# Transposing three token tiles by DMA instead of by matmul, with one mixer tile and two statistics moved, in an attention and mixer kernel

## The chip, the cores and the metric

The kernel runs on one core of one Trainium2 chip. The metric is the device time of one execution in microseconds; the median of three runs is given, and one more execution was taken by the hardware profiler. The engines are called PE (TensorE, matmuls), PEld (its weight loads), DVE (VectorE), ACT (ScalarE), POOL (GpSimd) and SP (SyncE, which here only issues DMAs; SPq is its queue).

## The reference

The input x has 2048 tokens of 512 channels. It is normalised, and the normalised tokens go two ways: through attention over cached keys and values, and through a mixer with an MLP, whose result gates the attention's.

```python
def _A_ref(x, k_cache, v_cache, wq, wo):           # 32 heads of 128, 2048 keys
    q = (x @ wq).reshape(B, Sq, H, Dh)              # then heads first
    p = _softmax(einsum("bhqd,bhkd->bhqk", q, k_cache) * Dh ** -0.5)
    return einsum("bhqk,bhkd->bhqd", p, v_cache) ... @ wo

def _B_ref(x, w1, w2, w3, w4):
    h = _gelu(_layernorm(x) @ w1)
    # four groups of 128 channels, shifted by +1, -1, +2 and -2 tokens
    x1 = x + concatenate([g0, g1, g2, g3]) @ w2
    return x1 + _gelu(_layernorm(x1) @ w3) @ w4     # 512 -> 1792 -> 512

xn = _layernorm(x)
out = x + _A_ref(xn, ...) * _silu(_B_ref(xn, ...))
```

All arrays are bf16.

## The kernel before

Tokens are cut into 16 tiles of 128 (index t). The kernel has a prologue of about 130 us, which computes the whole mixer with the MLP apart from held-back pieces, and then the attention: 128 units (a head with 512 queries each) of eight slots, each slot a pair of score matmuls, an exponential on ACT, and the value matmuls of an earlier slot. The diff touches only the first 50 us of the prologue.

Every engine executes its own instructions in the order in which the program issues them (`pin` keeps it). DMAs of SP are issued in order too; each also waits until the DMA eight places before it has landed, since eight completion semaphores are used in turn. So the order of work is the order of the Python lines, per engine.

The prologue's steps, by their functions:

- `load_x(t)` (L163) loads a token tile into a buffer of the tag "ta", of which there are ten. Tiles 0 to 7 are loaded first, then the query weights of four heads, then w2, then tiles 8 to 15.
- `ln1(t, tr)` issues on DVE the statistics of tile t + 1 (L182, L183, with two small POOL operations, L177 and L178, for the inverse root) and the normalisation of tile t into `xall` (L187), and then calls `tr(t)`, which puts the tile's transpose into `xnT`.
- `tr_pe(t)` does that with four 128-column matmuls against an identity matrix into a PSUM buffer "ps_o", and a copy by ACT (L201). `tr_dma(t)` does it with one DMA transpose from `xall` to `xnT`, issued by SP (L204).
- `m1(c0, 512)` is the mixer's first matmul for four tiles at once: two PSUM buffers of 1024 columns, eight matmuls each, and a gelu on ACT into `hT` (L215). It reads the four tiles' columns of `xnT`. For tiles 0 to 3 `m1_tile` does the same tile by tile.
- `m2(t)` is the second matmul of a tile: four matmuls from `hT`, shifted by up to two tokens, into a "ps_o" buffer, of which there are two (pool psO). `x1(t, ps)` adds it to `xall` on DVE (L227), and frees the buffer.
- `q_ahead(u)` computes the queries of a unit ahead of the attention: four matmuls (`q_mm`) into a buffer of pool psX, "xa" or "xm" in turn by the length of the list `made`, and a copy by ACT (`q_copy`, L279). The units of the last heads use weights `wq_e`, which SP loads (L594) after the DMA transposes of tiles 8 to 15; the weights w3 follow (L596).
- `stats(xall, mv2, rs2, t)` are the second statistics, of the mixer's result, and `ln2(t)` normalises with them and issues a DMA transpose into `xn2T` (L235) for the MLP's first matmul `m3` (L244).

Before the change, tiles 0 to 7 are transposed by `tr_pe` and 8 to 15 by `tr_dma`; `tr_q` puts one query unit of the first four ahead of each of the transposes of tiles 4 to 7. All loads of tiles 8 to 15 are issued before that. On PE the order from there on is: m2 of tiles 0 and 1, m1(512), units 4 to 7, m2 of tiles 2 and 3, m1(1024), four units with `wq_e`, m2 of tiles 4 to 7, m1(1536), m2 of tiles 8 to 10, three units, m2 of tiles 11 to 15, and then m3. On DVE the second statistics of tiles 4 to 7 stand between the residual adds of tiles 10 and 11.

Of the kernel before, what the change touches and what calls it, by code (L numbers as in the profile page):

```python
# [10 lines left out]
FP32 = mybir.dt.float32  # L11
# [6 lines left out]
def kernel(  # L18
# [15 lines left out]
    nc = tc.nc  # L34
    P = nc.NUM_PARTITIONS
# [3 lines left out]
    Sq, D = x2d.shape  # L39
# [6 lines left out]
    DC = D // P  # L46
# [17 lines left out]
    def pool(name, bufs=1, space=None, **kw):  # L64
        if space is not None:
            kw["space"] = space
        return tc.tile_pool(name=name, bufs=bufs, **kw)
# [4 lines left out]
    xall = const.tile([P, NT, D], BF16, name="xall")  # L72
# [5 lines left out]
    mv2 = const.tile([P, NT, nc.vector.BN_AGGR_DIM], FP32, name="mv2")  # L78
    rs1 = const.tile([P, NT], FP32, name="rs1")
    rs2 = const.tile([P, NT], FP32, name="rs2")  # L80
# [12 lines left out]
    psO = ent(pool("psO", 2, PSUM))  # L93
    psX = ent(pool("psX", 1, PSUM))
# [14 lines left out]
    def mm(out, lhsT, rhs, start, stop):  # L109
        pin(nc.tensor.matmul(out=out, lhsT=lhsT, rhs=rhs, start=start, stop=stop))  # L110
# [50 lines left out]
    def load_x(t, eng):  # L161
        xin[t] = tokp.tile([P, D], BF16, tag="ta", bufs=10, name="xin")
        pin(eng.dma_start(out=xin[t][:], in_=xsrc[t]))  # L163
# [11 lines left out]
    def rsqrt(out, var):  # L175
        ve = smp.tile([P, 1], FP32, name="ve")
        pin(nc.gpsimd.tensor_scalar(out=ve[:], in0=var, scalar1=EPS, scalar2=None, op0=ALU.add))  # L177
        pin(nc.gpsimd.tensor_tensor(out=out, in0=ve[:], in1=nhalf[:], op=ALU.pow))  # L178

    def stats(src, mv, rs, t):  # L180
        bn = smp.tile([P, nc.vector.BN_STATS_DIM], FP32, name="bn")
        pin(nc.vector.bn_stats(out=bn[:], in_=src))  # L182
        pin(nc.vector.bn_aggr(out=mv[:, t, :], in_=bn[:]))  # L183
        rsqrt(rs[:, t:t + 1], mv[:, t, 1:2])

    def norm_to(out, src, mv, rs, t):
        pin(nc.vector.tensor_scalar(  # L187
            out=out, in0=src, scalar1=mv[:, t, 0:1], scalar2=rs[:, t:t + 1],
            op0=ALU.subtract, op1=ALU.mult))
# [7 lines left out]
    def tr_pe(t):  # L197
        tp = psO.tile([P, DC, P], FP32, tag="ps_o", name="ps_o")
        for dc in range(DC):
            mm(tp[:, dc, :], xall[:, t, dc * P:(dc + 1) * P], ident[:], True, True)  # L200
        pin(nc.scalar.activation(out=xnT[:, :, t * P:(t + 1) * P], in_=tp[:], func=ACT.Identity))  # L201
# [4 lines left out]
    def m1(c0, w):  # L206
        for jp in range(DC // 2):
            b = BASE_J[2 * jp]
            ps = psS.tile([P, 2, 512], FP32, name="ps_s")
            for j in range(2):  # L210
                jc = 2 * jp + j
                for dc in range(DC):
                    mm(ps[:, j, 0:w], w1_sb[:, dc, jc * P:(jc + 1) * P],
                       xnT[:, dc, c0:c0 + w], dc == 0, dc == DC - 1)
            pin(nc.scalar.activation(  # L215
                out=hT[:, 2 * jp:2 * jp + 2, b + c0:b + c0 + w], in_=ps[:, :, 0:w],
                func=ACT.Gelu_apprx_tanh))

    def m2(t):
        ps = psO.tile([P, D], FP32, tag="ps_o", name="ps_o")  # L220
        for jc in range(DC):
            c0 = BASE_J[jc] + t * P - SHIFT[jc]
            mm(ps[:], hT[:, jc, c0:c0 + P], w2_sb[:, jc, :], jc == 0, jc == DC - 1)
        return ps
# [4 lines left out]
    def ln2(t):  # L229
        c, ts = divmod(t, 4)  # L230
        if ts == 0:
            xn2T[c] = pL.tile([P, DC, 512], BF16, tag="xn2T", bufs=2, name="xn2T")
        y = tokp.tile([P, D], BF16, tag="ta", bufs=10, name="xn2")
        norm_to(y[:], xall[:, t, :], mv2, rs2, t)
        pin(nc.sync.dma_start_transpose(out=xn2T[c][:, :, ts * P:(ts + 1) * P], in_=y[:]))  # L235
# [30 lines left out]
    def q_mm(u, dcs, tag="xa"):  # L266
        g, qt, hh = units[u]
        if dcs[0] == 0:
            st[u] = dict(psq=psX.tile([P, 512], FP32, tag=tag, name="ps_q"))
        for dc in dcs:  # L270
            mm(st[u]["psq"][:], wqs[g * HG + hh][:, dc, :],
               xnT[:, dc, qt * 512:(qt + 1) * 512], dc == 0, dc == DC - 1)

    def q_copy(u, eng=None):
        qT = qtp.tile([P, 512], BF16, name="qT")
        if eng is None:
            pin(nc.vector.tensor_copy(out=qT[:], in_=st[u].pop("psq")[:]))  # L277
        else:
            pin(nc.scalar.activation(out=qT[:], in_=st[u].pop("psq")[:], func=ACT.Identity))  # L279
        st[u]["qT"] = qT  # L280
# [251 lines left out]
    def ln1(t, tr):  # L532
        if t + 1 < NT:
            ln1_stats(t + 1)
        ln1_norm(t)
        tr(t)
# [28 lines left out]

    made = []

    def q_ahead(u):
        q_mm(u, range(DC), ("xa", "xm")[len(made) % 2])
        q_copy(u, nc.scalar)  # L570
        made.append(u)

    def tr_q(t):
        q_ahead(t - 4)
        tr_pe(t)

    for t in range(8, 16):
        load_x(t, nc.sync)
    for t in range(4, 8):
        ln1(t, tr_q)  # L580
    pend = [(t, m2(t)) for t in range(2)]
    for t in range(8, 12):
        ln1(t, tr_dma)
    m1(512, 512)
    for t, ps in pend:
        x1(t, ps)
    for u in range(HG, 2 * HG):
        q_ahead(u)
    pend = [(t, m2(t)) for t in range(2, 4)]
    for t in range(12, 16):  # L590
        ln1(t, tr_dma)
    for h in range((NG - 1) * HG, NG * HG):
# [9 lines left out]
    for u in range(NU - 2 * HG, NU - HG):  # L602
        q_ahead(u)
    for t in range(4, 8):
        x1(t, m2(t))
    for t in range(4):
        ln2(t)
    m1(1536, 512)
    for t in range(8, 11):
        x1(t, m2(t))  # L610
    for u in (2 * HG, NU - 1, NU - HG):
        q_ahead(u)
    for t in range(4, 8):
        stats(xall[:, t, :], mv2, rs2, t)
    for t in range(11, 16):
        x1(t, m2(t))
# [109 lines left out]
    for v in range(1, NU):  # L726
        if v not in made:
            for dc in range(DC):
                k = dc - 1 if v - 2 >= TURN.start else dc // 2
                q_plan[(v - 1) * SPU + k].append((v, (dc,)))  # L730

    for n in range(UB * SPU):
        u, p = divmod(n, SPU)
# [81 lines left out]
    def bank(pl, tag, **kw):  # L815
        return pl.tile([P, D], FP32, tag=tag, name="ps_w", **kw)[:]
# [4 lines left out]
    ps = {ts: bank(psW, "w") for ts in (0, 1)}  # L821
# [83 lines left out]
```

## Time and profile before

| what | value |
|---|---|
| median of three runs | 1252.07 us (1251.08 to 1252.3) |
| profiled execution, its own time | 1249.84 us |
| span of the profiled execution | 1248.0 us |
| mean granted PE clock | 0.999 |
| busy PE, ACT, DVE, POOL | 1241.3, 1111.2, 1007.5, 35.4 us |
| DMA, mean | 85 GB/s |
| m1(512), m1(1024), m1(1536) start on PE | 17.57, 26.23, 36.71 us |
| m3 of the first 512 tokens starts on PE | 50.23 us |
| first DMA transpose of `xnT` issued by SP | 15.09 us |
| first `wq_e` load issued by SP | 26.11 us |

Times inside the profile count from the start of the span. A row of a timeline gives start, length, engine, line and operation; PE's matmuls are pipelined, so rows of PE overlap by some tenths of a microsecond, and the pace is read from start to start. The chain that ended last is followed back from the end through what released each step.

### The profile page before, as it was taken

The page shows a single profiled execution, that of the slowest core. Times are in us where ns is not written, and L with a number is a line of the kernel's source. Part 1 is how long each engine was busy: PE and PEld are TensorE (multiplying, and loading weights), DVE is VectorE, ACT ScalarE, POOL GpSimd, SP SyncE. Part 2 cuts the span into 40 slices and gives each one's busy share as a digit, 9 for nine tenths or more (in the row PEclk, how much of TensorE's full clock was granted, in tenths as well). Part 3 has the DMA queues.
Part 4 walks back from the last instruction along what each step waited for, and adds up shares of the span by engine and source line. Part 5 has one row for each costly group of instructions (what it writes and reads, how often), then busy time and mean ns, then how long its engine had stood idle before and what let it go on. Part 6 is the DMA issues. An engine that isn't in the chain of part 4 may idle for free.

```text
span 1248.0 us, 16327 instructions
## 1 busy us (share of the span) xinstructions
PE 1241.3 (99%) x5884; PEld 606.2 (49%) x5884; DVE 1007.5 (81%) x1452; ACT 1111.2 (89%) x1117; POOL 35.4 (3%) x91
## 2 busy tenths in 40 slices
PE   9999999999999999999999999999999999999998
PEld 5444444444444444444444444444444444444444
DVE  7621678888888888888888888888888989899887
ACT  5344989999999999999999999999999999999997
POOL 5310000000000000000000000000000000000000
PEclk9999999999999999999999999999999999999999
DMA  6582023454244523553235524363245523462222
GB/s 179 116 149 64 18 43 72 89 111 85 49 96 89 116 52 65 97 120 68 68 86 105 102 40 93 81 119 68 60 98 103 103 67 82 102 117 60 60 65 60
DMA packets 235825, 106.48 MB, mean 85 GB/s; under 512 B 187808, under 2 KB 219040, under 8 KB 235744
## 3 DMA queue, kind: packets, MB, share of 16 engines
q1 hardware_dynamic: 234224, 102.82, 40.0%
q0 software_dynamic: 672, 1.84, 0.8%
q8 instruction: 46, 0.75, 0.3%
q10 hardware_dynamic: 848, 0.79, 0.2%
q14 instruction: 35, 0.29, 0.1%
HBM read 67.90 MB, written 2.36 MB: 56 GB/s over the span
## 4 chain that ended last, share of the span: by engine, by line
PE 99%; DVE 1%; ACT 1%; issue 0%; ACTq 0%
PE ps_s L110 40%; PE ps_o L110 38%; PE ps_wo L110 9%; PE ps_q L110 8%; PE ps_m L110 2%; PE ps_warm L110 0%; PE ps_oh L110 0%; ACT qT L279 0%; DVE bn L182 0%; ACT tb L501 0%; ACT xnT L201 0%; PE ps_w L110 0%; PE ps_sum L110 0%; DVE y L404 0%; DVE xall L227 0%
## 5 line engine op out<-in xcount | busy, mean ns | idle before, releaser
L293 ACT ACTIVATE pT<-ps_s 128x1024 bf16<-128x1024 f32 x1016 | 1037.4, 1025 | 61.8 <-PE ps_s L110 11.5
L110 PE MATMUL ps_s<-qT,kT 128*128 128x512 bf16 (+1 forms) x2064 | 609.1, 377 | 0.0
L110 PE MATMUL ps_o<-pT,vb 128*128 128x512 bf16 x2032 | 603.5, 379 | 0.0
L304 DVE TENSOR_TENSOR acc<-acc,pT 128x2048 bf16<-128x2048 bf16 x254 | 307.7, 1211 | 97.3 <-ACT pT L293 96.2
L110 PEld LDWEIGHTS <-kT 128*128 128x128 bf16 x2064 | 232.9, 113 | 218.0
L110 PEld LDWEIGHTS <-vb 128*128 128x128 bf16 x2064 | 201.8, 98 | 224.0 <-issue 0.5
L110 PE MATMUL ps_wo<-wo_h,oT 128*128 128x512 bf16 x496 | 186.7, 379 | 0.0
L299 DVE TENSOR_TENSOR acc<-pT 128x2048 bf16<-128x2048 bf16 x127 | 155.3, 1223 | 36.0 <-ACT pT L293 35.6
L110 PE MATMUL ps_q<-xnT,wq_h 128*128 128x512 bf16 x488 | 180.1, 379 | 0.0
L365 DVE TENSOR_TENSOR oT<-ps_o,rb 128x512 bf16<-128x512 f32 x127 | 86.7, 682 | 10.1 <-DMA rb<-dr 10.0
L308 DVE TENSOR_TENSOR acc<-acc 128x1024 bf16<-128x1024 bf16 x127 | 87.9, 692 | 4.3
L110 PEld LDWEIGHTS <-oT 128*128 128x128 bf16 x508 | 56.7, 112 | 58.6 <-issue 0.2
L345 DVE TENSOR_REDUCE sm<-tT 128x4 f32<-128x512 bf16 x116 | 78.6, 678 | 1.2 <-DMA tT<-acc 0.9
L277 DVE CAST qT<-ps_q 128x512 bf16<-128x512 f32 x113 | 77.2, 683 | 0.0
L110 PEld LDWEIGHTS <-wq_h 128*128 128x128 bf16 x488 | 47.6, 98 | 56.7 <-issue 0.2
L423 DVE TENSOR_TENSOR sacc<-ps_wo,sacc 128x512 f32<-128x512 f32 x96 | 65.6, 684 | 4.5 <-PE ps_wo L110 4.4
L314 DVE TENSOR_TENSOR acc<-acc 128x512 bf16<-128x512 bf16 x126 | 53.6, 425 | 4.3
L244 ACT ACTIVATE h2T<-ps_s 128x1024 bf16<-128x1024 f32 x28 | 28.7, 1025 | 24.3 <-PE ps_s L110 24.3
L110 PE MATMUL ps_s<-xn2T,w_sb 128*128 128x512 bf16 x224 | 48.8, 379 | 0.0
L110 PEld LDWEIGHTS <-w_sb 128*128 128x128 bf16 x336 | 30.4, 98 | 32.1
L110 PEld LDWEIGHTS <-h2T 128*128 128x128 bf16 x224 | 21.9, 98 | 26.3
L110 PE MATMUL ps_m<-w_sb,h2T 128*128 128x512 bf16 x112 | 33.3, 379 | 0.0
(74 smaller groups left out, 337.7 us busy)
## 6 DMA issues: line engine op xcount, KB each, us to landing
rb<-dr SPq DMA_DIRECT2D x127, 256.0 KB, 3.9
vb<-in_A_v_cache_dram SPq DMA_DIRECT2D x64, 256.0 KB, 3.0
wq_h<-in_A_wq_dram SPq DMA_DIRECT2D x32, 128.0 KB, 3.1
wo_h<-in_A_wo_dram SPq DMA_DIRECT2D x32, 128.0 KB, 2.8
w_sb<-in_B_w_dram SPq DMA_DIRECT2D x8, 256.0 KB, 5.1
kT<-in_A_k_cache_dram SPq DMA_TRANSPOSE x128, 3.0
xl<-in_A_x_dram SPq DMA_DIRECT2D x16, 128.0 KB, 3.5
dr<-rc SPq DMA_DIRECT2D x127, 2.0 KB, 1.4
```

Of the source, the lines that this page charges most:

```text
L110: pin(nc.tensor.matmul(out=out, lhsT=lhsT, rhs=rhs, start=start, stop=stop))
L244: pin(nc.scalar.activation(out=h2[c, f][:], in_=ps[:], func=ACT.Gelu_apprx_tanh))
L277: pin(nc.vector.tensor_copy(out=qT[:], in_=st[u].pop("psq")[:]))
L293: pin(nc.scalar.activation(out=s["pT"][-1][:, jj:jj + 2, :], in_=sps[:], func=ACT.Exp, scale=SCALE))
L299: pin(nc.vector.tensor_tensor(out=s["acc"][:], in0=s["pT"][0][:], in1=s["pT"][1][:], op=ALU.add))
L304: pin(nc.vector.tensor_tensor(out=a[:], in0=a[:], in1=st[u]["pT"][i][:], op=ALU.add))
L308: pin(nc.vector.tensor_tensor(out=a[:, 0:2, :], in0=a[:, 0:2, :], in1=a[:, 2:4, :], op=ALU.add))
L314: pin(nc.vector.tensor_tensor(out=a[:, 0, :], in0=a[:, 0, :], in1=a[:, 1, :], op=ALU.add))
L345: pin(nc.vector.tensor_reduce(out=sm[:], in_=s["tT"][:], axis=mybir.AxisListType.X, op=ALU.add))
L365: pin(nc.vector.tensor_tensor(out=to, in0=o, in1=rb, op=ALU.mult))
L423: pin(nc.vector.tensor_tensor(out=sa, in0=ps[:], in1=sa, op=ALU.add))
```

## The change

Tiles 4, 5 and 6 are transposed by `tr_dma` in place of `tr_pe`; tile 7 stays with PE. Of the loads of tiles 8 to 15, which SP issued all together, tiles 8 to 11 are still issued at once, 12 and 13 behind the DMA transpose of tile 4, and 14 and 15 behind that of tile 5; the transpose of tile 6 follows, and then those of tiles 8 to 15. So SP issues three more DMAs, and PE runs units 0 to 3 back to back.

m2 of tile 2 moves ahead of m1(512), into the psX buffer "xa"; its residual add moves along. Units 4 to 7 take "xm" and "xa" in the other order (the argument k). The second statistics of tiles 4 and 5 move ahead of m1(1536) and of the residual adds of tiles 8 to 10; those of 6 and 7 stay where they were.

```diff
-    def m2(t):
-        ps = psO.tile([P, D], FP32, tag="ps_o", name="ps_o")
+    def m2(t, pl=psO, tag="ps_o"):
+        ps = pl.tile([P, D], FP32, tag=tag, name="ps_o")
...
-    def q_ahead(u):
-        q_mm(u, range(DC), ("xa", "xm")[len(made) % 2])
+    def q_ahead(u, k=0):
+        q_mm(u, range(DC), ("xa", "xm")[(len(made) + k) % 2])
         q_copy(u, nc.scalar)
         made.append(u)
 
+    more_x = {3: range(8, 12), 4: range(12, 14), 5: range(14, 16)}
+
     def tr_q(t):
         q_ahead(t - 4)
-        tr_pe(t)
-
-    for t in range(8, 16):
-        load_x(t, nc.sync)
+        (tr_dma if t < 7 else tr_pe)(t)
+        for k in more_x.get(t, ()):
+            load_x(k, nc.sync)
+
+    for k in more_x[3]:
+        load_x(k, nc.sync)
     for t in range(4, 8):
         ln1(t, tr_q)
     pend = [(t, m2(t)) for t in range(2)]
+    pend.append((2, m2(2, psX, "xa")))
...
     for u in range(HG, 2 * HG):
-        q_ahead(u)
-    pend = [(t, m2(t)) for t in range(2, 4)]
+        q_ahead(u, 1)
+    pend = [(3, m2(3))]
...
     for t in range(4):
         ln2(t)
+    for t in (4, 5):
+        stats(xall[:, t, :], mv2, rs2, t)
     m1(1536, 512)
...
-    for t in range(4, 8):
+    for t in (6, 7):
         stats(xall[:, t, :], mv2, rs2, t)
```

## The prediction, on record before the change was run

> **What bounds the kernel now.** I read the page first, then the chain of waits for the first 52 us (the diff touches nothing later), the timelines of TensorE (PE) and of SyncE's queue (SPq) there, and the DMA landings.
>
> ```profile
> PE 1241.3 (99%) x5884; PEld 606.2 (49%) x5884; DVE 1007.5 (81%) x1452; ACT 1111.2 (89%) x1117; POOL 35.4 (3%) x91
> PE 99%; DVE 1%; ACT 1%; issue 0%; ACTq 0%
> ```
>
> PE is the bound: 99% busy, 99% of the chain. So a microsecond of PE work or PE idling taken away in the prologue moves all that follows, and whatever ends later than PE wants it costs the same. PE's timeline (start, length; a row's length overlaps the next, so I count from start to start):
>
> ```profile
> 11.24 1.03 PE L110 MATMUL ps_q<-xnT,wq_h 128*128 128x512 bf16 x4
> 12.11 0.39 PE L110 MATMUL ps_o<-ident,xall 128*128 128x128 bf16 x4
> 12.33 1.03 PE L110 MATMUL ps_q<-xnT,wq_h 128*128 128x512 bf16 x4
> ...
> 15.62 2.11 PE L110 MATMUL ps_o<-w_sb,hT 128*128 128x512 bf16 x8
> 17.57 3.62 PE L110 MATMUL ps_s<-xnT,w_sb 128*128 128x512 bf16 x16
> ...
> 45.42 1.89 PE L110 MATMUL ps_o<-w_sb,hT 128*128 128x512 bf16 x8
> 47.56 2.83 PE L110 MATMUL ps_o<-w_sb,hT 128*128 128x512 bf16 x12 [0.25 <-DVE xall L227]
> ```
>
> Four transposing matmuls of one tile take 0.22 us of PE (12.11 to 12.33), a query unit 0.87 (11.24 to 12.11), and one tile of the second mixer matmul, m2, also 0.87 (four 512-column matmuls). The last row shows PE idle for 0.25 us for VectorE's (DVE's) residual add. The chain there shows why: four second statistics stand ahead of that add.
>
> ```profile
> 46.13 0.59 DVE bn L182
> ...
> 46.84 0.68 DVE xall L227
> ```
>
> SP's queue, and where a DMA transpose is priced (least/median/most ns of issue, then us from issue to landing):
>
> ```profile
> 8.47 3.99 SPq L163 DMA_DIRECT2D xin<-in_A_x_dram  x8
> 15.09 10.97 SPq L204 DMA_TRANSPOSE xnT<-xall  x8
> 26.11 2.22 SPq L594 DMA_DIRECT2D wq_e<-in_A_wq_dram  x4
> ...
> L204 SPq DMA_TRANSPOSE xnT<-xall x8: 1196/1216/1300, 15.1 to 24.8; - x8
> DMA to landing us min/median/max: 2.4/2.5/2.7
> ```
>
> SP issues in order: a transposed tile holds it 1.2 to 1.3 us, a plain load about 0.5 (eight in 3.99), and the four extra query weights wq_e stand behind all transposes.
>
> **Part one: tiles 4 to 6 leave PE.** Removed: 12 matmuls and three ACT copies. On PE that is 3 x 0.22 = 0.66 us. Bounds: nothing, if PE had waited there for ACT anyway; 3 x 0.39 = 1.17 by the rows' lengths. ACT does run without a pause there (0.60 and 0.49 us alternating, 1.09 a pair, equal to PE's pitch), but each query copy begins 0.03 us after its matmuls end, so PE leads: 0.66. The short wait of m2(1) for tile 7's ACT copy stays, since q(3), tile 7 and m2(0) follow each other as before.
>
> *When the three tiles arrive.* m1(512) reads tiles 4 to 7 at once, so the last, tile 6, is what counts. PE gets there at 17.57 + 0.87 (the m2 tile now ahead of it) - 0.66 = 17.78. SP: load 11 is issued at 10.03 in 0.38; tile 4 (normalised by 10.34) at 10.45 to 11.75; loads 12 and 13 to 12.75; tile 5 at 12.8 to 14.05; loads 14 and 15 to 15.0; tile 6 at 15.05, landing 2.5 later at 17.55. The margin is 0.2 us. The wait for the eighth DMA back doesn't bind: tile 5 waits for w2, landed at 12.1. Behind PE's wait for tile 6 everything on PE is queued.
>
> *DMA engines.* Three tiles issued at 15.09, 16.49 and 17.78 make a share of 0.49 in 16 to 20 us: 4 x 0.49 / 3 = 0.65 us of all engines each.
>
> ```profile
> 8.00:12.00 4.00, 4.00 (x64) 3.58 (x62) 3.90 (x10) 3.42 (x10) 3.13 (x8) 1.00 0.98 271
> 12.00:16.00 4.00, 4.00 (x32) 2.29 (x30) 3.86 (x12) 3.80 (x8) 3.04 (x8) 1.00 0.63 196
> ```
>
> The share (before the GB/s) leaves 0.08 + 1.48 = 1.56 us free by 16 us: room for tiles 4 and 5, with tile 6 after. But they queue behind w2 and the loads, in engines that are full until 12, so I call d what tile 6 is late beyond 15.05 + 2.5. Bounds for d: 0, and 4.6 from the slowest rows of any transpose in backlog:
>
> ```profile
> 64.80 3.54 SPq L235 DMA_TRANSPOSE xn2T<-xn  x1
> 79.76 1.76 SPq L235 DMA_TRANSPOSE xn2T<-xn  x1
> ```
>
> There the issue took 3.54 and 1.76 us instead of 1.22, that is 2.3 or 0.55 more, for each of two tiles ahead of tile 6. At 79.76 two plain loads of 256 KB stood ahead on the same queue, as w2 and x loads do here, and it landed 3.6 after its issue; at 64.80 fourteen loads from GpSimd's queue shared the engines, which none does here. I take d = 0.1, since SP issues loads every 0.5 us from 8.5 to 11.8 although the engines are full.
>
> *SP's queue behind it.* Loads 12 to 15 come up to 2.4 us later; DVE wants load 12 at 17.34 and has it by 16. Tiles 8 to 11 go out at 16.35 to 20.25, wanted at 25.6: covered. Tile 12 then waits for its DVE normalisation (20.91, and 0.62 later for a third residual add ahead of it: 21.5); tiles 12 to 15 at 21.55 to 25.45, the first wq_e at 26.7 instead of 26.11. It landed in 2.4: 29.1. PE's weight load wanted it at 29.47, and now at 28.81. So 0.3 us is paid there, and d moves it one for one; the next three have 0.1 to 0.6 of slack.
>
> **Part two: m2(2) ahead of m1(512), in psX.** The same four matmuls, moved; m2(3) alone stays behind. Its columns end in tile 3, whose gelu is done at 12.1. It holds the psX buffer "xa" until DVE's third add (about 20.4); the swapped parity gives the next query unit "xm", and "xa" is wanted at 22.1. Cost nothing; if that add were late, PE would pay the lateness.
>
> **Part three: statistics of tiles 4 and 5 ahead of m1(1536).** Two pairs of 0.8 us move to DVE's idle stretch before the add of tile 8 (2.33 us of idle at 41.23). Then the add of tile 11 follows its matmuls, and of the 0.25 us idle about 0.05 stays: -0.20. GpSimd's two small operations per tile move along, idle there from 31 to 44 us.
>
> **Sum.** -0.66 - 0.20 + 0.30 + 0.10 = -0.46 us. On the profiled execution (span 1248.0, own time 1249.84) that gives 1249.4; the median of the runs shown is 2.23 higher, 1252.07, so 1251.6. It is 0.04%; about 0.2%, 2.5 us, is what a measurement of this kernel can tell from no change.
>
> **Rivals.**
>
> *Late tiles, a small loss or no gain (0.20).* The price of 79.76 for tile 4 alone gives d = 0.55 and a sum of 0.0; for tiles 4 and 5 with a landing of 3.6, d = 2.2 and +1.6: 1252.1 to 1253.7. For it: the full engines. Against: 2.4 to 2.7 in all eight rows of L204. The Trainium skill (VectorE: DVE Perf Modes, The three transpose paths and Rules for kernel authors) speaks against this change: TensorE where PSUM will do, at 390 ns a block, and the DMA crossbar at 1309 ns only otherwise. By its figure a tile of four blocks would be an estimated 5.2 us, tile 6 would land at 20.3, and the time would be 1254.2; the trace has 2.5 us for a tile.
>
> *SP blocks, slower (0.09).* If the engines' backlog holds the issue of tiles 4 and 5 as at 64.80, d is 4.6: PE waits 4.4 us for m1(512) and 0.5 for wq_e, +4.0, 1256.1. It counts as slower from d = 3.1, tile 6 landing after 20.6. For it: three of the four issues of L235 from 63 to 73 us took long (3.54, 1.82, 2.90). Against: only with GpSimd's loads in the air.
>
> *All cover holds, more gain (0.12).* wq_e lands in time too, or the matmuls cost their rows' lengths: -0.86 to -1.4, so 1250.7 to 1251.2.
>
> *A transpose is dearer on PE than it looks (0.04).* Tile 0's four, the first, have a row of 0.63 us: three tiles then take 1.9, the sum is -1.7, 1250.4. The Trainium skill (TensorE: Matmul & The Clock Gate, Part 4: PE-mode transpose) gives about 275 ns for each block in a kernel; 12 of them, 3.3 us by estimate, make the sum -3.1 and the time 1249.0, faster by 0.25%. The trace's 0.055 each (0.22 for four) is against it.
>
> **How the numbers follow.** Forecast 0.55; with the late tiles and the held cover 0.87 within 0.2%. Slower 0.09 is the blocked SP. Faster 0.04 is the dear transposes, counted in full though their row stays under the bound. The range takes -1.4 and +1.6 and 0.6 for the scatter of the runs (1251.08 to 1252.3), cut at the thin upper end: 1250.0 to 1253.7.
>
> **What would show it.** Right: PE starts m1(512) near 17.8 to 17.9 and the first wq_e matmul near 29.3 (29.69 before), no idle of 0.25 before m2's last tiles, and the last gated tiles about 0.5 us earlier. Wrong: an L204 issue over 1.5 us or a landing over 3 among the first three, a PE wait for DMA of a microsecond at 18 us or 29 us, PE idle on "xa", or any new wait of PE after 52 us.

## The result, and the profile after

The changed kernel takes 1253.89 us (median of 21 runs, 1252.77 to 1255.65); the kernel before, run beside it, 1251.35 (21 runs, 1250.44 to 1252.82). The ratio is 1.0019 (95% interval 1.0013 to 1.0025, given in brackets from here on): slower by 2.5 us, at the edge of the 0.2% that the prediction called measurable, outside its range and with the other sign. The profiled execution has a span of 1250.8 us (before 1248.0) and an own time of 1252.77; its mean granted clock is 0.999. The profiled execution of the kernel before (1249.84) was faster than every one of these 21 runs of it, so what its profile doesn't show can still cost the median run something.

The page's busy times and the shares of the chain that ended last:

```profile
PE 1234.7 (99%) x5757; PEld 606.0 (48%) x5872; DVE 1006.3 (80%) x1452; ACT 1108.9 (89%) x1114; POOL 35.5 (3%) x91
...
PE 93%; DVE 3%; DMA 3%; issue 1%; ACT 1%; POOL 0%; SPq 0%; ACTq 0%
```

PE has 99% of the chain in the kernel before and 93% here: the chain now runs through DVE and DMAs. The list of PE's waits has two lines that the kernel before doesn't have and that matter here (columns: us in total, times, longest):

```profile
PE ps_o L110 <- DVE oT L365: 1.7, 3, 0.7
...
PE ps_s L110 <- DMA xnT<-xall: 0.9, 1, 0.9
```

The second is the wait for tile 6. The first, three waits, lies in the attention, 200 us and more behind everything that the diff touches; no such line is in the profile of before. The 2.8 us between the two spans divide so: 0.56 by the start of the gated MLP matmuls (m3, 50.79 against 50.23), 1.65 in the three waits of the first line, 0.3 spread over the rest of the attention, and 0.3 behind PE's last matmul.

**The prologue.** PE's timeline:

```profile
15.07 3.00 PE L110 MATMUL ps_o<-w_sb,hT 128*128 128x512 bf16 x12
18.99 3.61 PE L110 MATMUL ps_s<-xnT,w_sb 128*128 128x512 bf16 x16 [0.92 <-DMA xnT<-xall]
...
30.50 3.75 PE L110 MATMUL ps_q<-xnT,wq_e 128*128 128x512 bf16 x16
...
46.32 4.64 PE L110 MATMUL ps_o<-w_sb,hT 128*128 128x512 bf16 x20
50.79 1.46 PE L110 MATMUL ps_s<-xn2T,w_sb 128*128 128x512 bf16 x6
```

m2(0) starts at 15.07 against 15.62, although tile 0 was 0.15 late in this execution, so the removed transposes gave 0.70. Twelve m2 matmuls later m1(512) finds tile 6 missing, and starts at 18.99. Three m2 tiles at the pace of the kernel before take 2.82 (1.95 for two there, 0.87 for the third) and would end at 17.89, so the loss is 1.10. The row of m2's last tiles has no idle inside it any more. SP's queue shows why tile 6 was late:

```profile
10.53 1.29 SPq L204 DMA_TRANSPOSE xnT<-xall  x1
11.87 1.89 SPq L163 DMA_DIRECT2D xin<-in_A_x_dram  x2
13.86 1.20 SPq L204 DMA_TRANSPOSE xnT<-xall  x1
15.11 1.05 SPq L163 DMA_DIRECT2D xin<-in_A_x_dram  x2
16.26 1.20 SPq L204 DMA_TRANSPOSE xnT<-xall  x1
```

The transposes are issued in 1.2 to 1.3 us, as priced, and tile 6 lands 2.69 after its issue. But the two loads behind tile 4 took 1.89 instead of about 1.0, so tile 5 went out at 13.86 (12.8 forecast) and tile 6 at 16.26 (15.05). The DMA engines, in windows of 1 us (columns PE, PEld, DVE, ACT, POOL, clock, DMA share, GB/s), and the queues from 12 to 13.5 us:

```profile
11.00:12.00 1.00, 0.95 (x12) 0.69 (x11) 0.96 (x4) 0.92 (x4) 0.74 (x3) 1.00 1.07 366
12.00:13.00 1.00, 1.00 (x6) 0.48 (x5) 0.96 (x4) 0.80 (x2) 0.76 (x2) 1.00 2.24 239
13.00:14.00 1.00, 1.00 (x7) 0.41 (x6) 0.97 (x4) 0.65 (x2) 0.81 (x2) 1.00 0.64 15
...
q8 instruction: 1, 0.02, 4.5%
```

From 13 to 14 us, with a transpose and loads still to be moved, the engines move 15 GB/s. In the packet records 25 packets of SP's queue, begun between 12.78 and 13.3, take 0.89 to 1.36 us each; the other 630 from 12 to 14 us take at most 0.06. The share above 1 a little earlier is these held packets, counted where they begin. At the head stands one packet of 16 KB on the queue q8: PE fetching its next instructions, from 12.31 us on, for 1.08 us. The second of the two loads, issued at 12.49, is the one that kept SP: 1.27 us in place of about 0.4.

**The attention.** The chain around the largest of the three waits:

```profile
256.02 1.75 DMA dr<-rc
...
257.87 5.46 DMA rb<-dr
...
263.35 0.70 DVE oT L365
...
264.10 0.59 PE ps_o L110 x2
```

A unit ends with the reciprocal of its softmax sums going out to memory (dr) and back, broadcast to all partitions (rb); DVE then writes oT, which frees the PSUM buffer "ps_o" for the next unit. rb took 5.46 us; the median in this profile is 4.1. The DMA view of 261 to 264 us, its rate in 40 slices and its queues:

```profile
GB/s 266 198 314 273 314 157 366 147 140 123 126 92 14 0 31 31 0 0 3 7 7 10 10 7 10 10 10 10 10 157 266 304 276 280 297 199 185 177 68 164
...
q8 instruction: 1, 0.02, 2.0%
```

From 261.9 to 263.1 nearly nothing moves, in the midst of a transposed load of keys and a plain load of values; again PE's fetch stands at its start (261.5). The other two waits (0.47 us at 679.14, 0.46 at 817.89) also end 2.6 us after the start of a fetch (676.51, 815.25). In the kernel before, the fetches around these places are at 256.5, 670.4 and 809.0. There they fall on dr, a step earlier, which takes 3.2 to 3.3 us; the rb behind it takes 3.3 to 3.4, and in that execution PE waits nowhere for oT.

PE's program is read in 46 such fetches of 16 KB (0.75 MB on q8), one in about 27.6 us. The change takes 24 instructions from it (12 matmuls and their 12 weight loads; 11746 in place of 11770), and 24 of 256 instructions are 2.6 of these 27.6 us. Against PE's own work the fetches do come later, by 2.2 us in the median; single ones by 0 to 4.7, and the three at the waits by 4.2 to 4.7. (Twice the weight loads that the profiles list gives 11744 and 11768, and two fewer than the text's number in the other kernels as well; the differences agree.) The Trainium skill (Runtime: NRT & Kernel Launch, Instruction fetch mechanics) says that instruction memory is refilled in blocks of 16 KiB, 256 instructions, and that crossing into the next is mostly hidden. The trace agrees on the block (11746 / 256 = 45.9). It agrees on the rest for PE, whose rows show no stop at a fetch itself; it doesn't for the other transfers, which the fetch can hold.

### The profile page after: what moved, and what is told of

It reads as the page before. It is cut to its first block, busy times and chain, and to the rows that moved or that the text cites. A ratio compares the mean times of both kernels' runs of the same rounds, so it can differ in the third digit from the quotient of the medians.

```text
span 1250.8 us, 16188 instructions
## 1 busy us (share of the span) xinstructions
PE 1234.7 (99%) x5757; PEld 606.0 (48%) x5872; DVE 1006.3 (80%) x1452; ACT 1108.9 (89%) x1114; POOL 35.5 (3%) x91
## 4 chain that ended last, share of the span: by engine, by line
PE 93%; DVE 3%; DMA 3%; issue 1%; ACT 1%; POOL 0%; SPq 0%; ACTq 0%
PE ps_o L110 37%; PE ps_s L110 37%; PE ps_wo L110 8%; PE ps_q L110 8%; PE ps_m L110 2%; DMA rb<-dr 1%; DVE acc L304 1%; DVE bn L182 0%; DMA dr<-rc 0%; ACT pT L293 0%; DMA vb<-in_A_v_cache_dram 0%; DVE oT L365 0%; DVE xall L187 0%; PE ps_oh L110 0%; DVE acc L308 0%
## 5 line engine op out<-in xcount | busy, mean ns | idle before, releaser
L293 ACT ACTIVATE pT<-ps_s 128x1024 bf16<-128x1024 f32 x1016 | 1036.5, 1024 | 64.6 <-PE ps_s L110 13.3
L110 PE MATMUL ps_s<-qT,kT 128*128 128x512 bf16 (+1 forms) x1969 | 588.6, 377 | 0.3
```

Source lines behind the costliest of these rows:

```text
L293: pin(nc.scalar.activation(out=s["pT"][-1][:, jj:jj + 2, :], in_=sps[:], func=ACT.Exp, scale=SCALE))
```

## The experiments

Each kernel was timed beside the kernel before. Five theories: **A**, the attention loses by where PE's fetches fall against its DMAs, so the number of PE's instructions decides; **B**, it loses by SP's new order in the prologue, handed on; **C**, tile 6 is late because of the DMA backlog, not of the fetch; **D**, more PE instructions are good as such; **E**, the kernels differ by their warming matmuls (matmuls at the start whose result nothing uses, to have PE at full pace when the first tile comes). The "attention" figure is the difference of the medians less the shift of m3's start in the profile, so it is a difference, where the expectations give the length of the attention in the profile. Since each ratio is known to some 0.1%, each such figure carries about 1 us: the pattern over the kernels counts, not the single one.

**Three kernels that tell A from B.** First, the kernel before with the change's number of instructions and none of its edits: its 12 warming matmuls are left out.

```diff
-    warm_mm(11)
...
-    warm_mm(1)
```

> The kernel before, without its 12 warming matmuls: 24 PE instructions fewer, the count of the kernel after, and nothing else. The first tiles run on a PE that has not been warmed, so the prologue may be 0 to 3 us longer; the verdict is the attention part, from the first exponential to the end. Theory A: it rises from 1122.7 to about 1124.9 us, with PE waits on DVE oT near 264, 679 and 818 us (plus the prologue's shift); time 1253.5 to 1257. Rival B: attention part 1122.7, no such waits.

1255.11 us against 1251.28, 1.0034 [1.0021, 1.0047]. Without the warming, two groups of m1_tile's matmuls take 1.91 us each in place of 1.06, and m3 starts 2.37 later (52.60); 1.46 remain for the attention. Its list of waits holds the line of the changed kernel:

```profile
PE ps_o L110 <- DVE xall L187: 6.4, 2, 5.9
PE ps_o L110 <- DVE oT L365: 1.6, 3, 0.7
```

So such waits come without any of the change's edits. They don't all come where they were expected: PE goes on at 542.6, 681.1 and 958.0. Second, the change's parts two and three alone, which leave the number at 11770.

```diff
+    pend.append((2, m2(2, psX, "xa")))
...
-        q_ahead(u)
-    pend = [(t, m2(t)) for t in range(2, 4)]
+        q_ahead(u, 1)
+    pend = [(3, m2(3))]
...
+    for t in (4, 5):
+        stats(xall[:, t, :], mv2, rs2, t)
     m1(1536, 512)
```

> The kernel before with only parts two and three of the change: m2 of tile 2 ahead of m1(512) in psX, and the statistics of tiles 4 and 5 moved ahead. All of tiles 4 to 7 are transposed by PE and the loads are in the old order; PE has 11770 instructions as before. Theory A and rival B alike: attention part 1122.7, prologue 0.2 to 0.3 us shorter (m3 starts at about 50.0 instead of 50.23), time 1251.0. If instead these moves cost, the attention part or the prologue rises.

1250.94, 0.9998 [0.9989, 1.0007]. m3 starts 0.18 earlier, as the -0.20 of part three had it, and nothing is left for the attention (-0.17), though its profile has two short waits for oT (0.5 us in all). Third, the changed kernel with its 24 instructions put back by cutting the warming into smaller matmuls.

```diff
-    def warm_mm(n):
+    def warm_mm(n, w=512):
...
-            mm(wps[:], warm[:, 0:P], warm[:], True, True)
+            mm(wps[:, 0:w], warm[:, 0:P], warm[:, 0:w], True, True)
...
-    warm_mm(11)
+    warm_mm(21, 256)
+    warm_mm(2, 128)
```

> The kernel after, with the 11 warming matmuls of 512 columns at the start cut into 21 of 256 and 2 of 128: the same columns, but 12 more weight loads and 12 more matmuls, so that PE has as many instructions (11770) as before the change. Everything else, SP's order included, is the kernel after. Theory A (PE's instruction fetches, 16 KB each, shifted by the 24 missing instructions, fall into DMA transposes and hold all DMA): the attention part, from the first exponential to the end, goes back from 1124.9 to 1122.7 us, the three PE waits on DVE oT (0.72, 0.47, 0.46 us near 264, 679 and 818) go, and the time is 1251.4 to 1252.2. Rival B (the three more DMAs and the later loads in SP's order, or the prologue's lateness, disturb the attention): attention part 1124.9 as it is, time 1253.9.

1252.96, 1.0014 [1.0005, 1.0023]; m3 at 51.40, so 0.51 for the attention in place of 1.97. Its profile, though, was of its slowest run (1253.82), and has the waits still:

```profile
PE ps_o L110 <- DVE oT L365: 1.9, 4, 0.7
```

The time is above the expected 1251.4 to 1252.2: for A by the medians, and not clean. Where the waits of this profile come from is taken up below the table.

**The same padding on the kernel before**, 11794 instructions (the edit is the one just shown).

> The kernel before with its 11 warming matmuls cut into 23 smaller ones of the same columns: 24 PE instructions more (11794). Theory A: the fetches move about 2.6 us earlier against the attention's work; the attention part may then be anything from 1121.5 to 1125, and where a PE fetch falls into a DMA transpose, DMA packets of 1 us and more are seen beside it. Rival B: nothing but the warming is touched, attention part 1122.7 within 0.3, time 1251.4.

1249.94, 0.999 [0.9981, 0.9999], though m3 starts 0.54 later: -1.88 for the attention. In its list of waits no line has oT; its longest wait is the 1.2 us at the start that the other kernels have too.

The kernel before loses something here as well, then, which its profile, of an unusually fast execution, doesn't show.

**The backlog, C.** In the changed kernel loads 8 to 15 all go ahead of the three transposes.

```diff
-    more_x = {3: range(8, 12), 4: range(12, 14), 5: range(14, 16)}
...
-        for k in more_x.get(t, ()):
-            load_x(k, nc.sync)
...
-    for k in more_x[3]:
+    for k in range(8, 16):
         load_x(k, nc.sync)
```

> The kernel after with SP's loads of tiles 8 to 15 all issued ahead of the DMA transposes of tiles 4 to 6, as in the old order of the loads; PE has 11746 instructions as in the kernel after. The transpose of tile 4 is then issued near 12.5 us, its packets run after 14 us, clear of the PE fetch at 12.3 to 13.4 us. Theory A: no packets of 1 us and more near 13 us, tile 6 issued at 15.1 to 15.3 instead of 16.26, PE's wait for it at most 0.2 instead of 0.92 us, m3 starts at 49.6 to 50.1 instead of 50.79; the attention keeps its waits: time 1252.6 to 1253.4. Rival C (the transposes are late because of the loads queued ahead of them): with eight loads ahead instead of four the wait is 0.9 us or more, m3 starts at 50.8 or later, time 1253.9 or more.

1253.44, 1.0012 [1.0003, 1.0021]. The windows and PE's timeline:

```profile
12.00:13.00 1.00, 1.00 (x6) 0.49 (x5) 0.96 (x4) 0.80 (x2) 0.74 (x3) 1.00 1.15 380
13.00:14.00 1.00, 1.00 (x7) 0.45 (x5) 0.96 (x4) 0.60 (x2) 0.82 (x2) 1.00 0.87 257
...
18.17 3.63 PE L110 MATMUL ps_s<-xnT,w_sb 128*128 128x512 bf16 x16 [0.15 <-DMA xnT<-xall]
...
30.74 0.60 PE L110 MATMUL ps_q<-xnT,wq_e 128*128 128x512 bf16 x2 [1.14 <-DMA wq_e<-in_A_wq_dram]
```

With only plain loads' packets moving, the same fetch (12.73 us) stops nothing (257 GB/s where the changed kernel has 15), and the wait for tile 6 falls from 0.92 to 0.15, with four more loads ahead of it. As the main cause C falls; a small part of it stays, since the issue of tile 4's transpose behind the eight loads took 1.85 us in place of 1.2 to 1.3. But m3 starts at 50.92, not at the 49.6 to 50.1 expected: wq_e landed 3.3 us after its issue, and its wait takes 1.14. The time is just above what A expected (1252.6 to 1253.4). The attention has +1.25, at 11746 instructions with SP's order changed again, which speaks for A.

**The changed kernel at 11794 instructions**: `warm_mm(35, 128)`.

> The kernel after, with the 11 warming matmuls of 512 columns cut into 35 of 128 (fewer columns in all, about as long on the cold PE): 24 pairs more, 11794 PE instructions, the count of before_pad12, which had no PE wait in its attention. Theory A: attention part 1122.1 to 1122.7 with no PE wait on DVE oT, prologue as in the kernel after (0.5 to 1.1 us over before), time 1250.0 to 1250.8, and runs closer together than the 2.9 us spread of the kernel after. Rival B (SP's new order does it): three waits or more in the attention, 1253 to 1254.

1251.02, 0.9996 [0.9987, 1.0005], with no wait for oT; the time is 0.2 above the expected range. It keeps SP's order whole and m3 is 0.74 late, yet the attention has -1.2. As a main cause B falls.

**The warming, E.** Here the 24 instructions are put back elsewhere: 12 matmuls of 128 columns, whose result nothing uses, in PE's wait for tile 6.

```diff
     pend.append((2, m2(2, psX, "xa")))
+    fill = psX.tile([P, 128], FP32, tag="xm", name="ps_fill")
+    for _ in range(12):
+        mm(fill[:], warm[:, 0:P], warm[:, 0:128], True, True)
```

> The kernel after, with 12 useless matmuls of 128 columns (0.65 us) put where PE waits 0.92 us for tile 6, ahead of m1(512); the start is untouched and PE has 11770 instructions, the count of before. Theory A: the attention's loss of 1.5 to 2 us goes although nothing was changed in the warming, the prologue stays as in the kernel after (m3 at 50.8 to 51.1): time 1251.6 to 1252.5. Rival E (the start's different warming, not the count, made the padded kernels faster): 1253.5 to 1254.5.

1252.79 against 1252.11 (15 runs) for the kernel before, run beside it: 1.0008 [0.9999, 1.0017]. The useless work fills the wait:

```profile
17.93 0.83 PE L110 MATMUL ps_fill<-warm 128*128 128x128 bf16 x12
18.86 1.46 PE L110 MATMUL ps_s<-xnT,w_sb 128*128 128x512 bf16 x6
```

The time lies a little above the expected 1251.6 to 1252.5, as the kernel before beside it does; m3 came earlier than expected, at 50.40. With the warming untouched, 24 added instructions made the kernel faster against its own kernel before (+0.68 in place of +2.54), and the attention has +0.51, as with the padded warming. That speaks against E, though the two intervals touch (1.0008 [0.9999, 1.0017] and 1.0019 [1.0013, 1.0025]). That both kernels with SP's new order and 11770 instructions have +0.5 where stats_m2 has -0.2 is what may be left of B; it is within the scatter.

**Cover for the keys.** If the loads of keys and values start two slots later, do they leave dr and rb alone?

```diff
-... (5, 7)[i % 2], lambda h=h, i=i: load_k(h, (i,)))
+... (7, 9)[i % 2], lambda h=h, i=i: load_k(h, (i,)))
...
-... * SPU + 6, lambda h=h, i=i: load_v(h, (i,)))
+... * SPU + 8, lambda h=h, i=i: load_v(h, (i,)))
```

> The kernel after with the attention's loads of keys (DMA transposes) and values issued two slots (2.2 us) later by SP; PE's instructions, their count (11746) and the prologue are those of the kernel after. Theory A: the fetches then meet other stretches of the key transposes, as they do in the kernel before, whose fetches come about 2.6 us earlier against the loads: the attention part falls from 1124.9 towards 1122.7, time 1252.0 to 1253.3. Rival B and rival D (the count as such): the attention's waits stay, time 1253.5 to 1254.2.

1298.99, 1.0376 [1.0362, 1.039]. The keys themselves come too late, 29.6 us of waits, and so the question isn't answered:

```profile
PE ps_s L110 <- DMA kT<-in_A_k_cache_dram: 29.6, 11, 5.0
```

**Versions meant to be fast.** Parts two and three with the warming as 23 matmuls of 192 columns (11794 instructions):

> Parts two and three of the change alone (all tiles 4 to 7 transposed by PE), with the warming matmuls cut into 23 of 192 columns: 11794 PE instructions. Theory A: prologue 0.2 us shorter to 0.2 longer than before (the 23 smaller ones may end a little later), no PE wait on DVE oT in the attention: time 1249.2 to 1249.9, faster than both kernels. Rival B: as stats_m2, 1250.9.

1249.76, 0.9988 [0.998, 0.9997]; m3 at 50.06. Then the whole change with the loads first, the four wq_e loads moved ahead of the transposes of tiles 12 to 15, and `warm_mm(35, 128)`:

```diff
-    for t in range(12, 16):
-        ln1(t, tr_dma)
...                                   # the wq_e loads
+    for t in range(12, 16):
+        ln1(t, tr_dma)
```

> The whole change, with the loads of tiles 8 to 15 issued ahead of the transposes of tiles 4 to 6, the four loads of wq_e ahead of the transposes of tiles 12 to 15, and the warming matmuls cut into 35 of 128 columns: 11794 PE instructions. Theory A: no PE wait over 0.2 us for tile 6 or wq_e, m3 starts at 49.3 to 49.8, no PE wait on DVE oT in the attention: time 1248.8 to 1249.5, the fastest of all. Rival C: the transposes are late behind eight loads, m3 at 50.5 or later, 1250.2 or more. Rival B: waits in the attention, 1252 or more.

1250.81, 0.9992 [0.9984, 1.0001]. The attention has -1.74, but m3 starts 1.06 late: the shorter warming leaves PE idle for 1.22 us ahead of the first tile, and the first two rows of m1_tile run at a half to two thirds of their pace (1.58 and 1.91 us for 16 matmuls of 128 columns, against 1.06), at a granted clock of 0.5 from 8.0 to 11.4 us. The time is 1.3 above the expected range. With `warm_mm(35, 160)` instead:

> As loads_wqe_pad24 (loads of tiles 8 to 15 first, wq_e ahead of the transposes of tiles 12 to 15, 11794 PE instructions), but with the 35 warming matmuls of 160 instead of 128 columns, so that PE is busy up to the first tile: in loads_wqe_pad24 it idled 1.22 us there and ran tiles 0 and 1 at half pace. Theory A: m1(512) starts at 17.9 to 18.3 us, m3 at 49.3 to 49.8, no PE wait on DVE oT: time 1248.7 to 1249.6, the fastest. Rival B: attention waits, 1251 or more.

1249.80, 0.999 [0.9982, 0.9999]. m3 starts at 49.57, 0.66 earlier than before; here all of the change's prologue pays, though the time is 0.2 above the expected range:

```profile
18.11 3.63 PE L110 MATMUL ps_s<-xnT,w_sb 128*128 128x512 bf16 x16 [0.23 <-DMA xnT<-xall]
```

Last, the kernel before with that warming, 11818 instructions, against D:

> The kernel before with its 11 warming matmuls cut into 35 of 160 columns: 48 PE instructions more than before (11818), 24 more than before_pad12. Theory A says that only where the fetches fall counts, so the steps of 1.5 us from 11746 to 11770 to 11794 need not go on: with no waits left in before_pad12 the time cannot fall much further, 1249.2 to 1250.2, or it rises again to up to 1252 as the fetches meet other transposes. A rival D, that more PE instructions as such make the attention faster in proportion, expects 1.6 us less than before_pad12: 1248.0 to 1248.6.

1249.99, 0.999 [0.9982, 0.9999]; attention -1.16 where 11794 gave -1.88. More instructions bring nothing as such, and D falls.

All in one table, the attention in us against the kernel before:

| PE's instructions | kernels | attention | mean |
|---|---|---|---|
| 11746 | after; before_cut12; after_loads_first | +1.97; +1.46; +1.25 | +1.6 |
| 11770 | before; stats_m2; after_pad12; after_fill12 | 0; -0.17; +0.51; +0.51 | +0.2 |
| 11794 | before_pad12; after_pad24; stats_m2_pad12; loads_wqe_pad24; best_pad24 | -1.88; -1.2; -1.56; -1.74; -0.73 | -1.4 |
| 11818 | before_pad24 | -1.16 | -1.2 |

The groups of 11746 and 11794 don't overlap, though each holds kernels with the order of SP before and after the change, and the shifts of m3 (-0.66 to +2.37) don't order them. So the time goes with the number of instructions. One limit stands: every kernel of 11794 and 11818 also has its warming cut up. At 11770 one has (after_pad12) and one hasn't (after_fill12), and both have +0.51.

The traces show how the fetches do it. The profiles of the three kernels with 11746 list seven waits for oT. At each a fetch begins within rb, which then takes 5.1 to 5.7 us (medians of 4.1 to 4.2). Those with 11770 list nine, and there the fetch comes 0.6 to 1.3 us after the issue of dr, which takes 3.2 to 3.6 us (medians of 1.4 to 1.5). Of after_pad12, with a fetch at 395.95:

```profile
395.18 3.33 DMA dr<-rc
...
398.59 4.08 DMA rb<-dr
...
402.69 0.70 DVE oT L365
```

So 24 instructions move a fetch from one step of this round trip to the other. In the four profiles with 11770, dr takes over 2.2 us in 61 of the 66 cases in which a fetch begins in it, and in 83 of the other 442. Of 55 transfers of rb over 5 us in the profiles of the thirteen kernels (all but after_kv_late2), 54 overlap a PE fetch. What stays open is why it costs nothing at 11794: there 25 transfers of rb in five profiles also take over 5 us, in other units, and no list of waits has oT.

stats_m2_pad12 and best_pad24 beat both kernels, by 0.1% the one before and by about 4 us the changed one. But the kernel before with cut warming alone does as well (1249.94 and 1249.99 against 1249.76 and 1249.80), so this gain goes with the count of instructions and not with the change, and the next edit to PE's program can undo it.

## Why the prediction was wrong

**Tiles off PE, -0.66:** right, 0.70.

**Idle ahead of m2's last tiles, -0.20:** right. 46.32 to 50.79 is 4.47 us, where 45.42 to 50.23 was 4.81: -0.34. In stats_m2 m3 is 0.18 earlier.

**m2(2) ahead, at nothing:** right; no wait on "xa" shows.

**wq_e, +0.30:** right in size. The first was issued at 27.98 and landed 2.47 later; PE started 0.25 later than the pace of its rows gives. Both stand later than forecast (26.7 and 29.3): tile 6 delayed SP and PE alike.

**d, +0.10: the step that failed in the prologue.** Measured, d is 1.4 (landing at 18.95, not 17.55), and cost PE 1.10. The text took 0.1 because SP's issues kept their pace while the engines were full. That held until 11.8 us and failed with the first transpose in flight, when the engines nearly stood still behind PE's fetch (15 GB/s): the load issued at 12.49 held SP for 1.27 us, and tile 6 went out 1.2 late. The rows of L235 that served as the upper bound (3.54 and 1.76 us of issue) were put down to backlog; the rival of late tiles, with 0.55 to 2.2 for d, names the right place and size and, in the main, the wrong cause, as after_loads_first shows. Its price is no error as such: no PE fetch lies near the row of 79.76 (the nearest are at 67.5 and 90.6), and tile 4's 1.85 in after_loads_first is of the same kind.

Together in the prologue: 0.15 (tile 0 late) - 0.70 + 1.10 + 0.25 - 0.34 = 0.46, and 0.1 in small pieces up to the 0.56 measured, in place of -0.46.

**Nothing later than 52 us, at nothing: the step that cost most.** "The diff touches nothing later" is right for the order of the work and wrong for the time: +1.97 of the 2.54 us arise there. A term was missing for what the removed instructions do to the rest of PE's program: they move its fetches, in the changed kernel onto rb (19 of 127 transfers of rb have a fetch begin in them, 6 before). The prediction's list of what would prove it wrong holds the sign that came, a new wait of PE after 52 us; none of its rivals has it.

**The other rivals:** SP blocked (d of 4.6) and all cover holding did not come. By the 0.70 for 12 transposes the dear transposes fall too; the Trainium skill's 275 ns for each (TensorE: Matmul & The Clock Gate) are 58 here. Of its 1309 ns a block by DMA (VectorE: DVE Perf Modes), which had tile 6 land 5.2 us after its issue, the trace has 2.69 for a tile of four blocks; its advice against the DMA transpose was right for this place by the outcome, not by its price.

## What to carry to other kernels

In a kernel whose bound engine is 99% busy and whose DMAs are covered by a microsecond or two, adding or taking away instructions moves the later instruction fetches, and here differences of 0.1 to 0.2% went with that alone: before crediting an edit with it, run the old kernel with the new number of instructions (here by cutting warming matmuls), and the new one with the old number. Look at the rate of the DMA engines in windows of 1 us around a late transfer; a hole with an instruction fetch at its head isn't a backlog, and the wait behind it shrank here although more loads went ahead. Where DMA transposes and plain loads are in flight together, give the transfer that something waits for closely 1 to 2 us of slack.

## What the runs showed of the hardware

A fetch of PE's instructions holds the other DMAs only beside a transpose. In the packet records of the thirteen profiles a hold is counted where at least 16 packets of SP's queue that begin within 1.5 us take over 0.9 us each. It is put to a fetch if it begins from 0.2 us before the fetch's start to 1.5 us behind it. A DMA of SP is in flight from its issue to its landing; dr and rb are plain ones:

| in flight when a PE fetch starts | fetches with a hold |
|---|---|
| transposes and plain DMAs | 81 of 271 |
| transposes alone | 0 of 32 |
| plain DMAs alone | 0 of 171 |
| neither | 0 of 124 |

The part of the transposes is firm. That of the plain DMAs is less so: without dr and rb among them, transposes alone have 7 of 123.

There are 122 holds in all, so 41 can't be put to a PE fetch in this way. A profile has between 2 (before_pad12, after_pad24) and 14 of them (the changed kernel), but stats_m2_pad12, the fastest, has 9 and the kernel before 12: what counts is whether one meets a dr or rb that is closely waited for. Why a fetch holds the other transfers isn't settled, and no run here tests it.
